# A retention and feed-forward kernel on Trainium2: new orders for its engines, and 13 activation transposes moved from TensorE to DMA

## The chip, the cores and the metric

The kernel runs on one core of a Trainium2 chip. The metric is device time in microseconds (us) of one execution. Before the change the median of three runs is 247.33 us (246.45 to 356.75). The core's engines are TensorE (PE; PEld is its weight load), VectorE (DVE), ScalarE (ACT), GpSimd (POOL) and SyncE (SP); each runs its own instruction list strictly in order. SP issues nearly all DMAs.

## The reference

The first half is retention: attention without softmax, with a decay per head and a causal mask. Its output, laid out as 4608 tokens by 512 features, goes through a feed-forward block with a softmax-weighted activation and a layer norm.

```python
scores = scale * np.matmul(q, k.transpose(0, 1, 3, 2))        # q, k, v: (8, 8, 576, 64) f32
gamma = 1.0 - 2.0 ** (-5.0 - np.arange(H))
ret = scores * np.where(rel >= 0, gamma[:, None, None] ** rel, 0.0)
x = (ret @ v), heads side by side                              # (4608, 512)
h = x @ w_in                                                   # (4608, 1024)
e = np.exp(h - h.max(-1));  solu = h * e / e.sum(-1)
ln = (solu - mean) / np.sqrt(var + 1e-6) * g_ln
out = ln @ w_out                                               # (4608, 512) f32
```

## The kernel before

**Tiles.** The 4608 tokens make 18 windows of 256 tokens. Attention works on 36 half windows `i` (256 tokens, four of the eight heads); the feed-forward block works on 36 tiles `t` of 128 tokens (all features). The kernel's steps have names with the number of the half window or tile behind them:

- SP: `ldq`, `ldk`, `ldv` load f32 inputs (256 KB each) into rings of five buffers; `out` stores a result tile in two or four DMAs.
- POOL: `sq`, `sk` scale q and k by the head's decay (line 308; the first two `sq` are on DVE); `cv` casts v (line 316); `sm` updates the running state `g` (line 441); `sc` casts it to f16 in two halves, `sbd` (line 450); `rs` is the power -0.5 of two tiles' variance (line 530).
- PE: `T` transposes q and k (line 325), `S` makes scores (383), `K` makes the new state term, `I` applies the old state, `V` applies the masked scores (all 348); `M1` is x @ w_in (468), `L` transposes the activation `solu` in eight 128x128 pieces into PSUM (536), `M2` is the product with w_out (560).
- DVE: `mask` (416), `sa` and `sd` (430 to 437, state sums), `em` (479, negated copy of h and its row minimum, the negated maximum), `so` (501, the product of hn and the exponentials, both f32 in SBUF), `x` (519 and 522, the statistics of a window's two tiles at once), `od` (568).
- ACT: `qe`, `xe`, `le` copy the PSUM results of `T`, of `V` and of `L` to SBUF (333, 456, 544); `ex` (491), `va` (510, sum of squares), `oe` (576, scaled result).

**Loops between engines.** The state makes a loop from half window to half window: `K` (PE) to `sa`, `sd` (DVE) to `sm`, `sc` (POOL) to `I` (PE), and the next `K` follows the `V` behind that `I`. A feed-forward tile runs `M1`, `em`, `ex`, `so`, then `L`, `le`, `M2`, `oe`, `out`. Rings limit how far an engine runs ahead: one PSUM buffer each for `xy`, `h_ps`, `o_ps`, `s_ps` and the transposes, three buffers for `solu`, four for `lnT`, three for `o_sb`.

**What sets the order.** `FIRST` holds one list per engine; an engine executes its steps in that order, whatever is ready. `order_ops` merges the five lists by the durations in `DUR` and the rings; this sets the order in which instructions are emitted, and hence which ring buffer each takes. Twelve warm-up products of zeros start PE (line 748); wherever the merge leaves a gap on PE before 31 us and before the first `M2`, further products of zeros are put (`WARM`, line 755).

SP's DMAs use eight semaphores in turn, so that a DMA is issued only once the eighth one before it has landed.

Of the kernel before, what the change touches and what calls it, by code (L numbers as in the profile page):

```python
# [18 lines left out]
    sq=1.03, sk=1.03, st_b=0.4, cast=0.84, rs=0.6, cv=0.61,  # L19
    ld=0.89, ldw=1.34, out=0.72, lm=0.42,  # L20
# [4 lines left out]
WARM = 31.0  # L25
NE = 14
WPOOL = ()

FIRST = dict(
    ACT=(  # L30
        "cv1 cv0 qe0 xe0 qe1 qe2 wi1a wi3a wi2a xe1 wi0a ex0 xe2 qe3 qe4 ex1 le0 xe3 qe5 wg6 va1 "
        "le1 wg2 wg0 wg4 xe4 ex2 nw va0 qe6 xe5 ex3 le2 oe0 va2 ex4 qe7 oe1 va3 qe8 xe6 qe9 xe7 "
        "oe2 le3 va4 ex5 oe3 le4 va5 qe10 xe8 ex6 xe9 le5 oe4 qe12 ex7 ex8 le6 oe5 qe11 xe10 va6 "
        "va7 le7 xe11 ex9 oe6 qe13 va8 va9 oe7 le8 xe12 ex10 qe14 ex11 xe13 le9 va10 oe8 qe15 "
        "ex12 xe14 le10 oe9 va11 qe16 va12 xe15 le11 oe10 ex13 qe17 ex14 qe18 oe11 xe16 va13 le13 "
        "va14 le12 xe17 ex15 qe19 oe13 le14 va15 qe20 ex17 xe18 oe12 qe21 ex16 xe19 oe14 qe22 "
        "va17 le15 va16 ex18 oe15 le16 le17 xe20 oe16 xe21 ex19 va18 qe23 va19 oe17 ex20 le18 "
        "xe22 qe24 ex21 xe23 oe18 le19 va21 le20 va20 oe19 qe25 xe24 ex23 qe26 oe20 xe25 ex22 "
        "le21 va23 qe27 va22 le23 oe21 le22 ex24 qe28 xe26 ex25 xe27 oe22 qe29 va24 va25 ex26 "
        "le24 oe23 qe30 xe28 le25 oe24 qe31 ex27 xe29 oe25 va26 qe32 va27 le26 ex28 le27 xe30 "  # L40
        "ex29 xe31 oe26 qe33 va28 va29 oe27 ex30 le28 ex31 xe32 qe34 xe33 oe28 qe35 va31 le29 "
        "va30 xe34 ex32 le30 xe35 ex33 oe29 va32 va33 ex35 oe30 le31 va35 le32 ex34 oe31 le35 "
        "va34 le34 oe32 oe35 le33 oe34 oe33"
    ),
    DVE=(
        "sq1 sq0 sa0 sd0 mask0 sa1 sd1 mask1 wi1b wi2b sa2 gc sd2 wi3b wi0b mask2 em0 sa3 sd3 so0 "
        "em1 mask3 wg7 so1 sa4 sd4 mask4 em2 wg1 wg5 wg3 mask5 sa5 em3 sd5 so2 x0 wp3 wp0 sa6 od0 "
        "sd6 mask6 em4 so3 od1 em5 sa7 sd7 mask7 so4 x1 od2 sa8 mask8 sd8 em6 od3 so5 sa9 mask9 "
# [12 lines left out]
        "T0 K0 S0 I0 V0 T1 K1 S1 T2 I1 S2 V1 K2 G M1_0 I2 V2 T3 K3 M1_1 T4 S3 L0 I3 V3 S4 K4 T5 "
        "M1_2 L1 I4 V4 K5 S5 M1_3 WM M2_0 T6 I5 V5 K6 S6 L2 M1_4 M2_1 T7 M1_5 I6 T8 V6 K7 S7 M2_2 "
        "T9 I7 V7 S8 K8 L3 M1_6 M2_3 I8 V8 K9 S9 L4 M1_7 T10 M2_4 I9 V9 K10 S10 L5 M1_8 T12 M2_5 "
        "L6 M1_9 T11 I10 V10 K11 S11 M2_6 L7 I11 V11 K12 S12 T13 M1_10 M2_7 I12 L8 V12 S13 K13 "
        "M1_11 T14 M2_8 I13 V13 K14 S14 L9 M1_12 T15 M2_9 L10 I14 V14 S15 K15 M1_13 T16 M2_10 I15 "
        "V15 S16 L11 M1_14 T17 M2_11 T18 I16 S17 V16 M1_15 L13 I17 V17 K18 S18 L12 M2_13 T19 "
        "M1_17 L14 I18 S19 V18 K19 T20 M2_12 M1_16 T21 M2_14 I19 V19 S20 K20 T22 M1_18 L15 I20 "
        "V20 S21 K21 M2_15 L16 M1_19 L17 M2_16 I21 V21 K22 S22 T23 M1_20 M2_17 I22 S23 V22 K23 "
        "L18 M1_21 T24 M2_18 I23 V23 S24 K24 L19 M1_23 L20 M2_19 T25 I24 M1_22 V24 K25 S25 T26 "
        "M2_20 I25 V25 S26 K26 L21 M1_24 T27 M2_21 L23 I26 V26 K27 S27 L22 M1_25 T28 M2_22 I27 "  # L70
        "V27 K28 S28 T29 M1_26 M2_23 L24 M1_27 T30 I28 V28 S29 K29 L25 M2_24 T31 I29 V29 K30 S30 "
        "M2_25 M1_28 T32 I30 V30 S31 K31 L26 M1_29 L27 M2_26 I31 V31 K32 S32 T33 M1_30 M2_27 "
        "M1_31 L28 I32 V32 S33 K33 T34 M2_28 I33 V33 S34 T35 M1_32 L29 I34 S35 V34 L30 M1_33 I35 "
        "V35 M2_29 M1_35 L31 M2_30 M1_34 L32 M2_31 L35 M2_32 L34 M2_35 L33 M2_34 M2_33"
    ),
    POOL=(
        "sk0 sm0 sc0 sk1 sk2 sq2 sm1 sc1 cv2 sm2 sc2 sq3 sk3 cv3 sk4 sq4 sm3 sq5 sc3 cv4 sk5 cv5 "
        "sm4 sc4 sk6 sq6 cv6 sm5 sc5 sk7 sk8 rs0 sq8 sq7 sm6 cv8 sc6 cv7 sq9 sk9 sm7 sc7 cv9 rs1 "
        "cv11 sk10 sm8 sc8 sq12 sq10 cv13 cv10 sm9 sc9 sk12 rs2 sq11 sm10 sc10 sk11 cv12 sq13 "
        "sq16 sk13 sm11 sc11 sq14 sk14 rs3 sm12 sc12 cv14 sm13 sc13 sq15 cv16 sk15 sm14 rs4 cv17 "  # L80
        "sc14 sk16 cv15 cv18 sm15 sc15 sq17 rs5 sk17 sk18 sq18 sq19 sk19 sq21 cv19 rs6 sk21 sk20 "
        "sm18 cv21 sc18 sq20 sq22 sk22 sm19 sc19 cv20 rs7 sm20 sc20 cv22 sk23 rs8 sq23 cv25 sm21 "
        "sk24 sc21 sm22 sq24 cv23 sc22 cv24 sk25 sq25 sm23 rs9 cv26 sc23 sk26 sq26 sm24 sq27 sc24 "
        "rs10 sm25 sc25 sq29 sk27 sm26 cv28 cv29 sc26 cv27 sk28 cv30 sq28 sk29 rs11 sm27 sc27 "
        "sq30 sq31 sk30 sk31 sm28 sc28 rs12 sq32 cv32 sm29 sc29 sq34 sm30 sc30 sk32 cv35 cv31 "
        "sk33 sm31 sq33 sc31 rs13 cv33 sq35 sk34 sm32 sc32 sk35 cv34 sm33 sc33 rs14 rs15 rs16 "
        "rs17"
    ),
    SP=(
        "ldk0 ldq1 ldv1 ldq0 ldv0 ldk1 lm ldv2 ldq2 ldk2 lwi3 lwi1 lwi2 lwi0 ldq3 ldk3 ldv3 ldk4 "  # L90
        "ldq4 ldq5 ldk5 ldv4 lwo6 ldv5 lwo0 lwo2 lwo4 ldk6 ldq6 ldv6 ldk7 ldv7 ldk8 ldq9 ldq8 "
        "ldq7 ldk9 ldv8 ldk10 ldq10 ldv9 out0 ldv11 ldv10 ldk12 ldq12 ldk11 ldv12 out1 ldv16 out2 "
        "ldv13 ldq16 ldq15 ldq13 ldk15 ldk14 out3 ldq11 ldk16 out4 ldk13 ldv17 ldv14 ldq14 ldk17 "
        "out6 ldq17 ldv15 ldq18 out5 ldq22 out7 ldv18 out8 ldk18 ldv21 ldv20 ldq19 ldk21 out9 "
        "ldk19 ldv19 ldk20 ldq21 ldq23 ldv22 ldv23 ldq20 ldk22 out11 out13 out10 ldk25 ldk24 "
        "ldv26 ldv25 ldq26 out12 ldk23 ldk29 ldv24 ldq25 ldv30 ldq24 ldk26 out14 out15 ldq27 "
        "out16 ldq31 ldk28 ldv27 ldv28 ldv29 out17 ldq28 ldv33 out18 ldk27 out19 ldq29 ldk31 "
        "ldq30 ldq32 ldv35 ldv31 ldk30 ldk33 out20 out22 ldq34 ldv32 ldk34 ldk32 out21 ldv34 "
        "ldq35 out23 ldk35 ldq33 out24 out26 out25 out27 out28 out29 out30 out31 out32 out35 "
        "out34 out33"  # L100
# [107 lines left out]
def kernel(  # L208
# [21 lines left out]
               xT=5, h=1, hn=3, e=2, oc=2, solu=3, sq=2, sml=8, lnT=4, o=1, osb=3)  # L230
# [52 lines left out]
    mhalf = small[:, 68:69]  # L283

# [156 lines left out]
    def state_cast(i):  # L443
        w, hf = divmod(i, 2)
        b, wi = wins[w]
        k = n_state[wi]
        n_state[wi] += 1
        s16 = sbd[wi][k % len(sbd[wi])]
        for e in range(2):
            nc.gpsimd.tensor_copy(out=s16[ee[e], :, :, ee[e]], in_=st[i]["g"][ee[e]])  # L450
        cur.setdefault((b, hf), {}).update({"g": st[i]["g"], wi: s16})
# [63 lines left out]
    def stats(w):  # L515
        d = ws[w]
        x = pools["sml"].tile([P, 2], FP, tag="w", name="w")
        d["x2"] = pools["sml"].tile([P, 2], FP, tag="w2", name="w2")
        nc.vector.scalar_tensor_tensor(  # L519
            out=x, in0=d["se"], scalar=1e-6, in1=d["se"], op0=ALU.mult, op1=ALU.mult  # L520
        )
        nc.vector.scalar_tensor_tensor(
            out=d["x2"], in0=d["sv"], scalar=float(DFF) ** -3, in1=x, op0=ALU.mult, op1=ALU.add
        )
# [7 lines left out]
    def ln_tp(t):  # L532
        d = tk[t]
        tp = pools["tp"].tile([P, 8, P], F16, tag="tp", name="tln")
        for c in range(8):
            nc.tensor.transpose(  # L536
                out=tp[:, c], in_=d["solu"][:, c * P : (c + 1) * P], identity=ident
            )
        d["tp"] = tp

    def ln_ev(t):
        d = tk[t]
# [245 lines left out]
```

## Time and profile before

| quantity | value |
|---|---|
| median of three runs | 247.33 us |
| the profiled execution | 246.69 us, span 244.9 us |
| mean granted TensorE clock | 0.992 |
| busy share PE / DVE / ACT / POOL | 88% / 75% / 70% / 71% |
| DMA moved | 42.62 MB, mean 174 GB/s |

The span reaches from the first to the last instruction; 1.8 us of the execution lie around it. The share of busy time is a mean over the whole execution: a fill stage of some 22 us, in which loads and weights arrive, then the stage in which attention and feed-forward steps of different tiles run side by side, then a tail from about 200 us on that is mostly feed-forward work. Matmuls are pipelined: a 128x512 product is recorded with 379 ns, while eight of them in a row take 1.73 us in the chain.

In an answer on one line of code, "x64: 386/398/1453" stands for 64 instructions with their shortest, median and longest time in ns. In the list of waits the three numbers are the total in us, the number of waits and the longest.

### The profile page before, as it was taken

Reading aid. Unit: us, or ns where it says so; the run is one execution under the profiler, and the core shown is the slowest. Engines: PE = TensorE matmul, PEld = TensorE weight load, DVE = VectorE, ACT = ScalarE, POOL = GpSimd, SP = SyncE. Lnnn points to the kernel's source line nnn. Section 1 sums busy time; section 2 is a strip of 40 time slices with the busy share of each in tenths; the row PEclk is TensorE's granted clock in tenths of the full one; section 3 lists DMA queues with packets and bytes.
Section 4 is the critical chain, followed back from the end, with each engine's and each line's share of the span. In section 5 each row is a group of like instructions: output and inputs, shape, how many; then the busy total and the mean of one; then the engine's idle time right before and its main releaser. Section 6 shows DMA issues by size and latency. Waiting matters only on the chain.

```text
span 244.9 us, 7426 instructions
## 1 busy us (share of the span) xinstructions
PE 214.4 (88%) x2998; PEld 124.1 (51%) x2998; DVE 182.9 (75%) x328; ACT 172.2 (70%) x301; POOL 172.7 (71%) x223
## 2 busy tenths in 40 slices
PE   8968887998997788999799889899869999999992
PEld 2435543554554445556456446455445554565550
DVE  7166899887995799989979767849845776897520
ACT  2234786767776597889769685868756687989971
POOL 2097994998959868799968969939995789631020
PEclk9999999999999999999999999999979999999999
DMA  7999999196886065798297865662516550510244
GB/s 188 322 367 300 352 295 269 30 246 170 226 236 185 3 170 175 193 305 237 63 256 196 264 175 136 170 172 82 178 29 188 156 150 4 129 46 23 65 94 120
DMA packets 65633, 42.62 MB, mean 174 GB/s; under 512 B 4024, under 2 KB 59456, under 8 KB 65600
## 3 DMA queue, kind: packets, MB, share of 16 engines
q1 hardware_dynamic: 65200, 41.96, 61.8%
q8 instruction: 23, 0.38, 0.6%
q10 hardware_dynamic: 400, 0.21, 0.4%
q14 instruction: 10, 0.08, 0.1%
HBM read 32.71 MB, written 9.44 MB: 172 GB/s over the span
## 4 chain that ended last, share of the span: by engine, by line
PE 33%; POOL 31%; DVE 13%; DMA 9%; issue 7%; ACT 5%; SPq 1%; POOLq 0%; DVEq 0%; ACTq 0%
POOL sbd L450 9%; PE h_ps L468 8%; POOL k L308 7%; PE o_ps L560 7%; POOL q L308 6%; PE xy L348 6%; POOL g L441 4%; DMA qr<-in_q_dram 4%; POOL v L316 3%; PE tln L536 3%; DVE ret L416 3%; DMA out_dram<-o_sb 2%; PE tqk L325 2%; DVE hn L479 2%; PE wm L755 2%
## 5 line engine op out<-in xcount | busy, mean ns | idle before, releaser
L468 PE MATMUL h_ps<-w_in,xT 128*128 128x512 f16 x288 | 68.8, 382 | 0.9 <-ACT w_in L612 0.9
L501 DVE SCALAR_TENSOR_TENSOR solu<-hn,e_sb 128x1024 f16<-128x1024 f32 x36 | 47.7, 1326 | 5.3 <-ACT e_sb L491 5.3
L479 DVE TENSOR_SCALAR_CACHE_REDUCE hn<-h_ps 128x1024 f32<-128x1024 f32 x36 | 43.8, 1218 | 9.9 <-PE h_ps L468 9.8
L491 ACT ACTIVATE e_sb<-hn,nm 128x1024 f32<-128x1024 f32 x36 | 41.4, 1151 | 8.0 <-DVE hn L479 6.2
L416 DVE TENSOR_TENSOR ret<-s_ps,masks 128x1024 f16<-128x1024 f32 x36 | 43.7, 1215 | 2.5 <-PE s_ps L383 2.5
L308 POOL TENSOR_TENSOR k<-kr,small 128x512 f16<-128x512 f32 x36 | 42.1, 1175 | 4.3 <-DMA kr<-in_k_dram 3.6
L510 ACT ACTIVATE sq<-solu,su 128x1024 f32<-128x1024 f16 x36 | 41.3, 1148 | 1.2 <-DVE solu L501 1.2
L308 POOL TENSOR_TENSOR q<-qr,small 128x512 f16<-128x512 f32 x34 | 39.4, 1165 | 3.7 <-DMA qr<-in_q_dram 3.0
L468 PEld LDWEIGHTS <-xT 128*128 128x128 f16 x288 | 27.0, 99 | 28.7 <-issue 2.0
L560 PEld LDWEIGHTS <-lnT 128*128 128x128 f16 x288 | 26.8, 98 | 28.7 <-issue 0.8
L441 POOL TENSOR_TENSOR g<-tt,small 128x128 f32<-128x128 f32 x32 | 17.1, 534 | 30.7 <-DVE tt L437 30.2
L560 PE MATMUL o_ps<-w2c,lnT 128*128 128x512 f16 x160 | 37.8, 379 | 0.1
L450 POOL CAST sbd<-g 64x256 f16<-64x256 f32 x64 | 34.8, 544 | 3.0
L456 ACT CAST xT<-xy 128x512 f16<-128x512 f32 x36 | 21.0, 584 | 21.3 <-PE xy L348 19.0
L333 ACT COPY qkT<-tqk 128x512 f32<-128x512 f32 x36 | 20.9, 579 | 15.4 <-PE tqk L325 15.3
L530 POOL TENSOR_TENSOR rs<-w,small 128x2 f32<-128x2 f32 x18 | 15.2, 846 | 20.3 <-DVE w L519 12.7
L348 PE MATMUL xy<-qkT,sbd 128*128 128x128 f16 (+1 forms) x128 | 13.5, 214 | 16.4 <-POOL sbd L450 15.8
L316 POOL CAST v<-vr 128x512 f16<-128x512 f32 x34 | 27.1, 801 | 0.8 <-PE xy L348 0.2
L560 PE MATMUL o_ps<-w2g,lnT 128*128 128x512 f16 x112 | 26.5, 379 | 0.6 <-DVE oc L568 0.6
L544 ACT COPY lnT<-tln 128x512 f32<-128x512 f32 x36 | 20.8, 577 | 5.7 <-PE tln L536 5.4
L536 PE MATMUL tln<-ident,solu 128*128 128x128 f16 x288 | 22.1, 220 | 0.5 <-ACT qkT L333 0.4
L536 PEld LDWEIGHTS <-solu 128*128 128x128 f16 x288 | 17.9, 98 | 6.5 <-issue 0.8
(53 smaller groups left out, 260.1 us busy)
## 6 DMA issues: line engine op xcount, KB each, us to landing
kr<-in_k_dram SPq DMA_DIRECT2D x32, 256.0 KB, 5.3
qr<-in_q_dram SPq DMA_DIRECT2D x32, 256.0 KB, 5.1
vr<-in_v_dram SPq DMA_DIRECT2D x32, 256.0 KB, 5.0
out_dram<-o_sb SPq DMA_DIRECT2D x64, 128.0 KB, 2.4
w_in_f<-in_moe_w_in_dram SPq DMA_DIRECT2D x4, 512.0 KB, 6.6
w_f<-in_moe_w_out_dram SPq DMA_DIRECT2D x4, 512.0 KB, 6.6
vr<-in_v_dram SPq DMA_DIRECT2D x16, 64.0 KB, 3.1
qr<-in_q_dram SPq DMA_DIRECT2D x16, 64.0 KB, 2.0
```

The lines of the kernel that those rows point to most:

```text
L308: eng.tensor_tensor(out=t.rearrange("p j h d -> p h j d"), in0=st[i][nm + "r"], in1=g_of(i, base), op=ALU.mult,)
L316: copy(out=t, in_=st[i]["vr"])
L348: nc.tensor.matmul(start=(c, e) not in begun, stop=False, skip_group_check=True, **kw)
L416: nc.vector.tensor_tensor(out=d["ret"].rearrange("p e h j q -> p (e h) (j q)"), in0=d["s"].rearrange("p e h j q -> p (e h) (j q)"), in1=ma ...
L450: nc.gpsimd.tensor_copy(out=s16[ee[e], :, :, ee[e]], in_=st[i]["g"][ee[e]])
L468: nc.tensor.matmul(out=h_ps[:, hh], lhsT=st[2 * w + dc // 2]["xT"][:, c, dc % 2], rhs=w_in16[:, dc, hh], start=(dc == 0), stop=(dc == 3),)
L479: nc.vector.tensor_scalar(out=d["hn"], in0=d["h"], scalar1=-1.0, scalar2=None, op0=ALU.mult, op1=ALU.min, accum_out=d["nm"],)
L491: nc.scalar.activation(out=d["e"], in_=d["hn"], func=ACT.Exp, scale=-1.0, bias=d["nm"], accum_out=ws[w]["se"][:, c : c + 1],)
L501: nc.vector.scalar_tensor_tensor(out=d["solu"], in0=d["hn"], scalar=1.0, in1=d["e"], op0=ALU.mult, op1=ALU.mult, accum_out=ws[w]["su"][:, ...
L510: nc.scalar.activation(out=x, in_=tk[t]["solu"], func=ACT.Square, scale=-float(DFF), bias=ws[w]["su"][:, c : c + 1], accum_out=ws[w]["sv"] ...
L536: nc.tensor.transpose(out=tp[:, c], in_=d["solu"][:, c * P : (c + 1) * P], identity=ident)
L560: nc.tensor.matmul(out=d["o"], lhsT=d["lnT"][:, c], rhs=(w2g16 if t < NE else w2c16)[:, c], start=(c == 0), stop=(c == 7))
```

## The change

It has four parts.

1. All five lists of `FIRST` are new.
2. For tiles 20 to 32 (`XBAR`) step `L` is one DMA with transpose, from `solu` to `lnT`, both in SBUF, issued by SP in the place that `L` has in SP's list. The eight PE transposes and the ACT copy `le` of those 13 tiles go. `M2` of these tiles waits for the DMA, and so does the reuse of the `solu` buffer.
3. `x` is done for each tile by itself with `tensor_scalar`, whose second factor is a column given as a scalar, in place of one `scalar_tensor_tensor` for two tiles with two SBUF tensors; the ring `sml` has 16 buffers in place of 8. `rs` still serves two tiles.
4. The zero products behind the first twelve are 11, at given places (`FILL`), in place of those in the merge's gaps. The table of durations gets two entries (one is for a step that is not used, since `CASTD` is empty).

```diff
-WARM = 31.0
+FILL = dict(T0=2, S0=1, I0=5, T2=1, T3=2)
+XBAR = tuple(range(20,33))
+CASTD = ()
 FIRST = dict(
     PE=(
-        "T0 K0 S0 I0 V0 T1 K1 S1 T2 I1 S2 V1 K2 G M1_0 I2 V2 T3 K3 M1_1 T4 S3 L0 I3 V3 S4 K4 T5 "
...
-        "V35 M2_29 M1_35 L31 M2_30 M1_34 L32 M2_31 L35 M2_32 L34 M2_35 L33 M2_34 M2_33"
+        "G T0 S0 K0 I0 T1 V0 K1 S1 T2 I1 V1 S2 K2 T3 M1_0 I2 V2 K3 S3 M1_1 I3 V3 K4 T4 M1_2 L0 S4 "
...
+        "S34 T35 M1_32 M2_29 I34 S35 V34 M1_33 I35 V35 M2_31 M1_35 L33 M2_30 M1_34 M2_33 L35 "
+        "M2_32 L34 M2_35 M2_34"
     ),
     SP=(
-        "ldk0 ldq1 ldv1 ldq0 ldv0 ldk1 lm ldv2 ldq2 ldk2 lwi3 lwi1 lwi2 lwi0 ldq3 ldk3 ldv3 ldk4 "
...
+        "ldv2 ldk1 ldk0 ldq0 ldk2 ldv0 ldq1 ldv1 lm ldq3 lwi0 ldq2 lwi2 lwi1 ldk3 lwi3 ldv3 ldk4 "
...
+        "out11 ldq27 out13 ldk26 ldv24 ldk24 ldv25 out14 out15 ldq26 out12 ldk27 ldq29 ldv27 "
+        "ldk29 ldk28 ldv26 out16 ldq28 ldq30 ldv28 out17 ldk30 ldq35 L20 ldq31 L21 ldv29 ldq33 "
+        "ldv30 ldv35 ldk31 ldq34 out18 out19 L22 out20 L23 ldk32 out21 ldv31 ldk33 ldk35 L24 L25 "
+        "ldk34 ldq32 out22 ldv33 out24 L26 out23 ldv32 L27 ldv34 L28 L29 out25 out27 out26 L31 "
+        "L30 out29 L32 out28 out30 out31 out33 out32 out35 out34"
     ),
 )
-               xT=5, h=1, hn=3, e=2, oc=2, solu=3, sq=2, sml=8, lnT=4, o=1, osb=3)
+               xT=5, h=1, hn=3, e=2, oc=2, solu=3, sq=2, sml=16, lnT=4, o=1, osb=3)
-    def stats(w):
+    def stats(t):
+        w, c = divmod(t, 2)
         d = ws[w]
-        nc.vector.scalar_tensor_tensor(
-            out=x, in0=d["se"], scalar=1e-6, in1=d["se"], op0=ALU.mult, op1=ALU.mult
-        )
-        nc.vector.scalar_tensor_tensor(
-            out=d["x2"], in0=d["sv"], scalar=float(DFF) ** -3, in1=x, op0=ALU.mult, op1=ALU.add
+        col = slice(c, c + 1)
+        nc.vector.tensor_scalar(
+            out=x, in0=d["se"][:, col], scalar1=d["se"][:, col], scalar2=1e-6,
+            op0=ALU.mult, op1=ALU.mult,
+        )
+        nc.vector.tensor_scalar(
+            out=d["x2"][:, col], in0=d["sv"][:, col], scalar1=float(DFF) ** -3, scalar2=x,
+            op0=ALU.mult, op1=ALU.add,
         )
+    def ln_dma(t):
+        d = tk[t]
+        d["lnT"] = pools["lnT"].tile([P, 8, P], F16, tag="lnT", name="lnT")
+        nc.sync.dma_start(out=d["lnT"], in_=d["solu"], transpose=True)
+        if t in XBAR:
+            op(f"L{t}", "SP", "ldt", [f"so{t}"], (m + 1, 4.9), lambda t=t: ln_dma(t), [("lnT", [f"M2_{t}"])])
+        else:
+            op(f"L{t}", "PE", "L", [f"so{t}"], (m + 1, 4.9), lambda t=t: ln_tp(t), [("tp", [f"le{t}"])])
+            op(f"le{t}", "ACT", "le", [f"L{t}"], (m + 2, 0.97), lambda t=t: ln_ev(t), [("lnT", [f"M2_{t}"])])
```

## The prediction

> **What bounds the kernel now.** I read the page's busy shares first, then the chain that ended last, the groups, the waits, and last the timeline and the windows of two places. No engine is full, and the chain wanders between PE (33%) and POOL (31%):
>
> ```profile
> PE 214.4 (88%) x2998; PEld 124.1 (51%) x2998; DVE 182.9 (75%) x328; ACT 172.2 (70%) x301; POOL 172.7 (71%) x223
> ...
> PE 33%; POOL 31%; DVE 13%; DMA 9%; issue 7%; ACT 5%; SPq 1%; POOLq 0%; DVEq 0%; ACTq 0%
> ...
> L450 POOL CAST sbd<-g 64x256 f16<-64x256 f32 x64 | 34.8, 544 | 3.0
> ...
> L544 ACT COPY lnT<-tln 128x512 f32<-128x512 f32 x36 | 20.8, 577 | 5.7 <-PE tln L536 5.4
> ```
>
> In order of time the chain is POOL and the state loop from 12 us to about 180 us, and almost purely PE from 200 to 240 us. Over 20 to 200 us the windows add up to 158.5 us of PE and 149.5 us of POOL in 180; from 200 to 220 PE has 19.4 of 20. So there are two stages: a loop between engines, then a PE queue.
>
> The answers on single lines show what lengthens the loop:
>
> ```profile
> L450 POOL CAST sbd<-g x64: 386/398/1453, 13.0 to 214.4; 64x256 f16<-64x256 f32 x64
> ...
> L441 POOL TENSOR_TENSOR g<-tt,small x32: 393/399/1379, 12.5 to 213.5; 128x128 f32<-128x128 f32 x32
> ...
> L308 POOL TENSOR_TENSOR k<-kr,small x36: 1036/1042/2108, 4.2 to 210.8; 128x512 f16<-128x512 f32 x36
> ...
> L501 DVE SCALAR_TENSOR_TENSOR solu<-hn,e_sb x36: 1208/1225/2058, 25.9 to 232.5; 128x1024 f16<-128x1024 f32 x36
> ```
>
> Each has a tight median and a longest case about 1 us beyond it; for POOL that is about one `so` of 1.225 us, for `so` about one `sk`. At 204.6 us the timeline has `so` (1.23 us) and `rs` starting together, and `rs` records 1.75 us where its median is 0.689. DVE's product and POOL's work take turns. Count against median over all POOL rows: 175.7 us recorded (42.1 + 39.4 + 27.1 + 17.1 + 34.8 + 15.2) less 144.3 us (36 x 1.042, 34 x 1.042, 34 x 0.609, 32 x 0.399, 64 x 0.398, 18 x 0.689) is 31.4 us of waiting inside POOL instructions. Of it, 13.6 us fall on `sm` and `sc`: (17.1 - 12.8) + (34.8 - 25.5). Those stand in the state loop, and PE pays:
>
> ```profile
> PEld L348 <- POOL sbd L450: 22.0, 20, 3.1
> ...
> PE xy L348 <- POOL sbd L450: 15.8, 17, 2.6
> ```
>
> The exclusive pair itself needs 144.3 + 36 x 1.225 = 188 us between 4 and 236 us, so 44 us of slack are there for a better order; PE is only a little less loaded.
>
> **The parts, against the profiled execution's 246.69 us** (its span is 244.9; 1.8 lie around it; the median shown is 247.33, which is 0.6 above).
>
> *1a. The fill.* T0 starts late only because zero products stand before it:
>
> ```profile
> 7.50 0.69 DVE L308 TENSOR_TENSOR q<-qr,small 128x512 f16<-128x512 f32 x1 [1.63 <-DMA qr<-in_q_dram]
> ...
> 10.92 0.39 PE L325 MATMUL tqk<-ident,q 128*128 128x128 f16 x4
> ```
>
> q0 is fourth in SP's list before and after, and lands at 7.5; `sq0` ends at 8.2, and T0 stood behind 23 zero products until 10.9. k0 goes from first place to third; third place landed at 6.6 (the v cast of 6.58), so `sk0` (1.04 us) ends at 7.6, in time. T0 can start near 8.2. What follows is the first state loop: v0, now sixth, gives `cv0` near 9.8 and K0 with it (11.46 before); `sc0` ends near 12.2 (2.36 us behind K0, as before). POOL then has `sq3`, `cv2`, `sq2` (2.7 us, from loads in places 1, 10 and 12) ahead of `sm1`, `sc1` (1.2 us), which end near 16.6 with q2's landing near 14.3 (18.36 before). xe1 and a weight cast are what M1_0 waits for, as before; it comes at about 19.8 in place of 21.47. **-1.7 us.** Ends: 0 (two more loads are ahead of the weights, at 0.75 us each by the 350 GB/s of that stretch, and `lm`, the masks, moves from seventh to ninth place) and -2.7 (all of T0's gain).
>
> *1b. The clock.* 45 zero products become 23, so PE idles more in the fill. One idle time of that size is in the trace: PE waits 2.58 us until 179.45, and the windows from 180 to 183 show
>
> ```profile
> 181.00:182.00 1.00, 1.00 (x9) 0.86 (x9) 0.99 (x1) 0.80 (x3) 1.00 (x2) 0.50 0.00 0
> ```
>
> half the clock for some 3.9 us; an M1 in it is recorded with 2.59 us in place of 1.89. One such spell costs up to 1.9 us of PE. In the fill PE has little to do, so I take **+1.0**; ends 0 and +3 (T, K, S, I, V of three half windows at half speed, 3 x 1.0 us more). The Trainium skill (TensorE: Matmul & The Clock Gate, Why this matters for your kernels) asks for no idle gaps above about 3 us and speaks of one window of idle; by it the gaps of 1 to 2 us that I expect would cost nothing, while the row says that 2.6 us, after a sparse stretch, were enough.
>
> *1c. The orders in the steady stage.* The trace can't show the new lists' waits. At best no `sm` or `sc` meets a `so`: -13.6 us, all on the loop and near PE's 15.8 us of waiting. At worst the new lists make as many new waits as they remove, and some more: +5 (the longest single waits of PE, POOL on `sd` and DVE are 2.6, 7.2 and 3.6 us; one or two such). POOL and DVE are both over 70% busy, so not every meeting can be avoided; I take half, **-6.8**.
>
> *2. L by DMA.* Removed: 13 x 8 transposes, 0.45 us per tile in the chain, and 13 `le` at 0.577 us (7.5 us of ACT). PE is the queue from 199.5 us on; the last ten L stand there, in the old list those of tiles 26 to 35 (the order at its end is L31, L32, L35, L34, L33), so seven of the thirteen are on the path: **-3.2**. The other six (2.7 us) lie where PE has idle time; I count none, and -5.9 is the end. Behind the last M1 the old list keeps PE 5 x 1.73 + 4 x 0.45 = 10.45 us, the new one 4 x 1.73 + 2 x 0.45 = 7.8: these are part of the same 3.2, with one M2 moved ahead. Late next is then em, ex, so, L, le, M2 of tile 34 (5.9 us from M1's end to M2_34 by the old timeline), against 6.1 us of PE work before it: balanced.
>
> Added: 13 DMAs on SP, each a hop of its own between `so` and M2. Nothing like them is in the trace. Nearest rows, 256 KB each as here:
>
> ```profile
> kr<-in_k_dram SPq DMA_DIRECT2D x32, 256.0 KB, 5.3
> ...
> qr<-in_q_dram SPq DMA_DIRECT2D x16, 64.0 KB, 2.0
> ```
>
> Cheap end 2.0 us to landing (the smallest row), dear end 19 us: the queue's 65200 packets took 61.8% of 16 x 244.9 us, 37 ns each, and in 32-byte pieces there would be 8192, over 16 engines. I take 5.3. M2 can stand it: between so20 and M2_20 the PE list holds some 14 us of work. Tighter is the `solu` ring of three: so25 needs tile 23's buffer. L23 stands behind out20 on SP, and so it is issued about 3.6 us after M2_20's end (the `oe` 0.7, a transpose, two stores 1.1), while so25 is ready some 7.5 us after it (T28, four attention steps, M2_21 and M1_25 are 4.8, em25 1.3, ex25 1.35). 5.3 us are too long by 1.4 there, with DVE 25% idle to take it up: **+0.5** for all such places; ends 0 and, at 19 us, +24 by the second rival's price. What is queued behind an L that waits: on SP the loads and stores (L29 ahead of out25, L31 ahead of L30 and out29). Loads are far ahead (after the fill POOL hardly waits for one), and no store there is needed within its L's wait.
>
> The Trainium skill (VectorE: DVE Perf Modes, The three transpose paths) speaks against this edit: 390 ns on TensorE against 1309 ns by DMA for one 128x128. Eight in series would be an estimated 10.5 us; no row shows it. With it, L23 would be late by 6.6 us in place of 1.4; with the 0.5 grown in proportion, to 2.4, the sum would be 238.4.
>
> *3. x by tile.* 36 old instructions recorded 12.5 us, 5.2 at their shortest of 0.144. Now 72; the nearest row, the `tensor_scalar` of `gln`, took 0.157: 11.3 us if nothing blocks them, 25 us at the old 0.35. That is -1 to +12 us of DVE, not on the path but near 200 us; **0**.
>
> Sum: 246.7 - 1.7 + 1.0 - 6.8 - 3.2 + 0.5 = **236.5 us**.
>
> **Rivals.**
>
> *The orders bring nothing* (the change doesn't do what it says). For it: nothing holds an engine back when the other runs; the lists only fix a sequence, and each of POOL's six rows can meet `so` at another place. Then 236.5 + 6.8 + 1.0 (part of 1a lost in the same waits) = 244.3, within 2%.
>
> *The transposes are slow*; the slower side. Place: `so(t+3)`, through the ring of three. Three tiles last 3 x 5.9 = 17.7 us (M1 from 21.5 to 229.3 over 35 tiles); `so` takes 1.3 and SP's queue some 3 (four 32-partition loads took 2.03), so it decides from 13.4 us to landing on. Price: 13/3 x (landing - 13.4); at 18 us +20, or 256. For it: the dear end, and that they share a queue with 40 MB of loads. Against: 256 KB usually land in 5.3 us. The 2% line is crossed at 17 us.
>
> *A dearer loop*: the worst end of 1c, 236.5 + 11.8 = 248.3, and 250.3 with 1b at its end.
>
> **How the numbers follow.** Forecast 0.57 (own range 229 to 242), orders bring nothing 0.22 (244), slow transposes 0.15 (256), dearer loop 0.06 (250). Low end of the range: 1a and 2 at their best with 11 of 1c's 13.6 give 246.7 - 2.7 - 5.9 - 11 + 0.5 = 228; all at its best at once is left out, some 0.05. High end: 254 takes in the dearer loop and leaves out the upper two thirds of the slow transposes, 0.1. 2%, about what a measurement of this kernel can tell from no change, is 242.4 to 252.3 around the median. Faster is the forecast's 0.57; within 2% are 0.22 and a third of the dearer loop, 0.24; slower are 0.15 and the rest of it, 0.19.
>
> **What would show it.** Right: T0 near 8.2 and M1_0 near 20 us; the means of `sbd` and `g` near 0.45 us (0.54 now); PE's waits for `sbd` halved; the DMA issues' row for `lnT` at 4 to 7 us; no wait of DVE's `so` on a landing above 2 us; PE's last product 2.5 us closer to the last M1. Wrong: `sbd`'s mean unchanged; `lnT` landing above 13 us with `so` or M2 waiting for it; clock 0.5 in the slices behind 8 us, with M1_0 no earlier than before; SP late with stores so that `oe` waits for its buffers.

## The result, and the profile after

The changed kernel takes **229.74 us** (median; fastest 227.68), the kernel before 247.82 us beside it: ratio **0.9255 [0.918, 0.9331]**. In a second set of runs the pair gave 230.75 against 247.15 us, ratio 0.932 [0.9249, 0.939]. The forecast was 236.5 us, so the time lies in its range, but the gain is 16 to 18 us where 10 to 11 were expected. The profiled execution takes 227.68 us (span 225.9, granted clock 1.0); it is the shortest of them. The medians given as measured take in every execution; the ratios, the table of experiments 3 and 4 and the differences of experiments 6 and 8 leave out those over 1.5% longer than the kernel's fastest.

The page of the changed kernel, the same rows as shown of before (line numbers have moved: `sbd` 450 to 451, `g` 441 to 442, `so` 501 to 504, the state products 348 to 349):

```profile
PE 200.7 (89%) x2872; PEld 115.4 (51%) x2872; DVE 182.9 (81%) x364; ACT 165.7 (73%) x288; POOL 167.5 (74%) x223
...
PE 38%; POOL 22%; DMA 14%; SPq 10%; ACT 5%; DVE 4%; issue 4%; ACTq 0%; POOLq 0%; DVEq 0%
...
L451 POOL CAST sbd<-g 64x256 f16<-64x256 f32 x64 | 31.4, 490 | 2.8
...
L442 POOL TENSOR_TENSOR g<-tt,small 128x128 f32<-128x128 f32 x32 | 17.2, 536 | 6.8 <-DVE tt L438 5.2
```

and the row of the new DMAs in the list of DMA issues, which ends with the median us from issue to landing:

```profile
lnT<-solu SPq DMA_TRANSPOSE x13, 3.3
```

POOL's share of the chain falls from 31% to 22%; DMA and SP's queue grow in it from 9% and 1% to 14% and 10%. The means of `sbd` and `g`, which the prediction wanted at 0.45 us, hardly move: 0.544 to 0.490 and 0.534 to 0.536. The answers on single lines:

```profile
L451 POOL CAST sbd<-g x64: 387/401/1387, 12.0 to 195.5; 64x256 f16<-64x256 f32 x64
...
L442 POOL TENSOR_TENSOR g<-tt,small x32: 393/400/1380, 11.6 to 194.6; 128x128 f32<-128x128 f32 x32
...
L504 DVE SCALAR_TENSOR_TENSOR solu<-hn,e_sb x36: 1209/1292/1986, 27.2 to 214.0; 128x1024 f16<-128x1024 f32 x36
```

DVE's product and POOL's pieces still meet. Count against median over `sm` and `sc` is (17.2 - 32 x 0.400) + (31.4 - 64 x 0.401) = 10.1 us, 13.6 before. But the waits say that fewer of these meetings reach PE:

```profile
PEld L349 <- POOL sbd L451: 11.6, 13, 2.1
PE xy L349 <- POOL sbd L451: 8.4, 12, 1.6
```

15.8 us of PE's waiting for `sbd` have become 8.4. POOL's own wait for DVE's `tt` fell from 30.2 to 5.2 us, and DVE's for PE's `h_ps` from 9.8 to 1.9.

**Where the 19.0 us between the two profiled executions lie.** The row of M1 gives its first and last start, here before the change and then after it:

```profile
L468 PE MATMUL h_ps<-w_in,xT x288: 376/379/634, 21.5 to 229.3; 128*128 128x512 f16 x144
```

```profile
L471 PE MATMUL h_ps<-w_in,xT x288: 376/379/390, 19.3 to 211.1; 128*128 128x512 f16 x144
```

The start is 2.2 us shorter, the stretch from the first M1 to the last 16.0 us (207.8 to 191.8), and what follows it, up to the end of the span, 0.8 us (15.6 to 14.8). So nearly all of it comes out of the middle. There the windows from 20 to 200 us, before and then after (PE's busy time first), show the same PE doing 10 us more work in 180:

```profile
20.00:200.00 180.00, 158.50 (x2367) 93.93 (x2366) 147.04 (x251) 130.78 (x228) 149.45 (x187) 0.99 0.67 187
```

```profile
20.00:200.00 180.00, 168.47 (x2520) 98.92 (x2519) 160.32 (x307) 141.17 (x247) 153.53 (x201) 1.00 0.79 207
```

### The profile page after: what moved, and what is told of

Its sections match the earlier page's. It is cut to its first block, busy times and chain, and to the rows that moved or that the text cites. A ratio compares the mean times of both kernels' runs of the same rounds, so it can differ in the third digit from the quotient of the medians.

```text
span 225.9 us, 7231 instructions
## 1 busy us (share of the span) xinstructions
PE 200.7 (89%) x2872; PEld 115.4 (51%) x2872; DVE 182.9 (81%) x364; ACT 165.7 (73%) x288; POOL 167.5 (74%) x223
## 4 chain that ended last, share of the span: by engine, by line
PE 38%; POOL 22%; DMA 14%; SPq 10%; ACT 5%; DVE 4%; issue 4%; ACTq 0%; POOLq 0%; DVEq 0%
PE o_ps L574 14%; PE h_ps L471 12%; POOL sbd L451 6%; PE xy L349 6%; DMA vr<-in_v_dram 6%; SPq L294 4%; DMA w_f<-in_moe_w_out_dram 4%; POOL k L309 4%; POOL v L317 4%; DMA w_in_f<-in_moe_w_in_dram 3%; POOL q L309 3%; POOL g L442 3%; PE tqk L326 3%; POOL rs L539 3%; ACT xT L459 2%
## 5 line engine op out<-in xcount | busy, mean ns | idle before, releaser
L309 POOL TENSOR_TENSOR k<-kr,small 128x512 f16<-128x512 f32 x36 | 45.0, 1257 | 13.0 <-DMA kr<-in_k_dram 11.2
L504 DVE SCALAR_TENSOR_TENSOR solu<-hn,e_sb 128x1024 f16<-128x1024 f32 x36 | 49.5, 1379 | 2.6 <-ACT e_sb L494 2.4
L309 POOL TENSOR_TENSOR q<-qr,small 128x512 f16<-128x512 f32 x34 | 36.9, 1090 | 0.9 <-DMA qr<-in_q_dram 0.3
L451 POOL CAST sbd<-g 64x256 f16<-64x256 f32 x64 | 31.4, 490 | 2.8
L539 POOL TENSOR_TENSOR rs<-w,small 128x2 f32<-128x2 f32 x18 | 16.3, 904 | 20.5 <-DVE w L530 10.2
L334 ACT COPY qkT<-tqk 128x512 f32<-128x512 f32 x36 | 20.8, 579 | 13.7 <-PE tqk L326 13.6
L317 POOL CAST v<-vr 128x512 f16<-128x512 f32 x34 | 24.6, 725 | 7.2 <-DMA vr<-in_v_dram 6.8
L442 POOL TENSOR_TENSOR g<-tt,small 128x128 f32<-128x128 f32 x32 | 17.2, 536 | 6.8 <-DVE tt L438 5.2
L590 ACT ACTIVATE o_sb<-o_ps,rs 128x512 f32<-128x512 f32 x20 | 13.7, 687 | 8.7 <-POOL rs L539 3.6
L326 PE MATMUL tqk<-ident,q 128*128 128x128 f16 x144 | 14.0, 220 | 3.1 <-DVE q L309 2.2
L349 PEld LDWEIGHTS <-sbd 128*128 128x128 f16 x128 | 8.3, 98 | 15.4 <-POOL sbd L451 11.6
```

The lines of the kernel that those rows point to most:

```text
L309: eng.tensor_tensor(out=t.rearrange("p j h d -> p h j d"), in0=st[i][nm + "r"], in1=g_of(i, base), op=ALU.mult,)
L317: copy(out=t, in_=st[i]["vr"])
L349: nc.tensor.matmul(start=(c, e) not in begun, stop=False, skip_group_check=True, **kw)
L451: (nc.vector if i in CASTD else nc.gpsimd).tensor_copy(out=s16[ee[e], :, :, ee[e]], in_=st[i]["g"][ee[e]])
L504: nc.vector.scalar_tensor_tensor(out=d["solu"], in0=d["hn"], scalar=1.0, in1=d["e"], op0=ALU.mult, op1=ALU.mult, accum_out=ws[w]["su"][:, ...
```

## The experiments

Line numbers below are each kernel's own. Ratios are against the kernel before on the same chip. Experiments 1 to 4 ran on one chip (before: 246.47 us), 5 to 8 on another (247.17), 9 and 10 with the changed kernel again on a third (247.15), 11 on a fourth (247.36).

**1. All of the change but the DMA transposes.**

```diff
-XBAR = tuple(range(20,33))
+XBAR = ()
-        "ldk29 ldk28 ldv26 out16 ldq28 ldq30 ldv28 out17 ldk30 ldq35 L20 ldq31 L21 ldv29 ldq33 "
+        "V23 S24 K24 L19 M1_23 T25 M2_18 T26 I24 S25 V24 K25 L20 M1_22 L21 M2_19 I25 V25 K26 S26 "
+        "le19 va19 qe25 va21 qe26 ex23 oe18 le20 xe24 va20 le21 oe19 xe25 va23 ex22 qe27 oe20 ex24 "
```

The lines are one each of SP's, PE's and ACT's lists; the other tiles go the same way.

> The new orders with all 36 L on TensorE again: the 13 transposes by DMA are undone, and the 13 L and le are put back into the lists of PE and ACT where they fit best. Theory A (the prediction's: seven of thirteen L on the path): 229.7 + 3.2 = 233 us. Rival B (with the new lists PE has hardly a gap anywhere, so each L counts): 13 x 0.45 = 5.9 us and more, 235.6 to 237 us. Rival C (the DMA transposes are most of the whole gain): 240 us or more.

Measured: 229.65 us, 0.9339 [0.9282, 0.9395], below all three expectations. By medians the DMA transposes are worth nothing (229.65 us without them, 229.74 and 230.75 with them), by ratios 0.2% (against the second pair above) to 0.8%. The orders, with the fill and x, give nearly everything.

PE is busy 206.9 us here and 200.7 in the changed kernel, but its idle time is 20.9 us here (of a span of 227.8) and 25.2 there. POOL's waits for loads, which bear on part 2, are here

```profile
POOL k L308 <- DMA kr<-in_k_dram: 7.5, 4, 5.0
...
POOL v L316 <- DMA vr<-in_v_dram: 6.1, 4, 3.4
```

and in the changed kernel

```profile
POOL k L309 <- DMA kr<-in_k_dram: 11.2, 4, 5.3
...
POOL v L317 <- DMA vr<-in_v_dram: 6.8, 4, 3.3
```

**2. The DMA transposes alone.** `L20` to `L32` are put into the old SP list where their `so` is ready; all else as before.

```diff
+XBAR = tuple(range(20, 33))
+        if t in XBAR:
+            op(f"L{t}", "SP", "ldt", [f"so{t}"], (m + 1, 4.9), lambda t=t: ln_dma(t), [("lnT", [f"M2_{t}"])])
...
-        "out16 ldq31 ldk28 ldv27 ldv28 ldv29 out17 ldq28 ldv33 out18 ldk27 out19 ldq29 ldk31 "
+        "ldv27 ldv28 ldv29 out17 L20 ldq28 L21 ldv33 out18 ldk27 out19 ldq29 ldk31 ldq30 ldq32 L23 "
```

> The old orders, with only the 13 L moved to DMA (the thirteen L and le leave the lists of PE and ACT, the DMAs go into SP's list where so is ready). Theory A: seven L leave the PE queue of the tail, 247.8 - 3.2 = 244.6 us; the orders are the larger part of the gain. Rival C: 240 us or less, the orders bring little. If the transposes hold up SP's loads and stores: 247 us or more.

Measured: 249.7 us, 1.0059 [1.0014, 1.0105], a small loss. The profiled execution is a long one (250.34 us, the ten lie between 245.8 and 251.78), with 13.7 us at half clock where the kernel before had 3.4. PE's 13 x 8 transposes are gone, but its busy time is no less (214.7 us, 214.4 before) and its idle time is more (33.8, 30.5 before). The timeline of PE near 204 us:

```profile
207.73 0.29 PE L346 MATMUL xy<-qkT,sbd 128*128 128x128 f16 x2 [3.89 <-POOL sbd L448]
```

and the chain of that time:

```profile
201.77 3.59 DMA qr<-in_q_dram
205.35 0.07 issue
205.42 1.46 POOL q L306
206.88 0.35 POOL sbd L448
```

A load of q, issued at 201.77 behind loads, stores and transposes on SP, holds `sq`, `sc` and with them PE for 3.89 us. That the 0.6% is lost in this place in the other executions is not shown.

**3 and 4. The exclusion taken away, before and after.** The product of two SBUF tensors becomes one that reads a single tensor.

```diff
-        nc.vector.scalar_tensor_tensor(
-            out=d["solu"], in0=d["hn"], scalar=1.0, in1=d["e"], op0=ALU.mult, op1=ALU.mult,
+        nc.vector.tensor_scalar(
+            out=d["solu"], in0=d["e"], scalar1=1.0, scalar2=None, op0=ALU.mult, op1=ALU.add,
```

> The kernel before with the product's operands changed: so reads only the exponentials (tensor_scalar times 1.0 with the sum), not hn; the output is another one, the instruction has the same size. With one SBUF input it should not exclude GpSimd, and every POOL row's mean falls to its median (0.40 for sbd and g, 1.04 for k). Theory A (the waits of sm and sc behind so are 13.6 us of the loop, and the new orders took half of it away): about 236 us, and the same step in the changed kernel brings half as much. Rival B (the orders' gain has little to do with the exclusion): the same step brings about as much in the changed kernel as here.

> The changed kernel with the same product of one SBUF input (another output, the same size). Theory A: the new orders have already put the products beside harmless POOL work, so at most -3 us, about 227 us. Rival B: the exclusion costs as much as in the kernel before, -6 us or more, 224 us or less.

Measured: in the kernel before 234.12 us, 0.9431 [0.9356, 0.9506]; in the changed kernel 226.0 us, 0.9154 [0.9085, 0.9222]. The answers on the two lines in the kernel before with one tensor read:

```profile
L501 DVE TENSOR_SCALAR_CACHE_REDUCE solu<-e_sb x36: 1203/1210/1221, 26.5 to 220.6; 128x1024 f16<-128x1024 f32 x36
...
L450 POOL CAST sbd<-g x64: 388/398/861, 13.6 to 202.5; 64x256 f16<-64x256 f32 x64
```

The product lasts as long as at its shortest before, but its longest case, 2.06 us, is gone, and POOL's six rows add up to 146.3 us in place of 175.7: the prediction counted 144.3 from medians. So it is this product's second operand from SBUF that shuts POOL out. `mask`, which also multiplies two tensors, but has one of them in PSUM, is never lengthened in the kernel before:

```profile
L416 DVE TENSOR_TENSOR ret<-s_ps,masks x36: 1209/1214/1225, 12.7 to 219.2; 128x1024 f16<-128x1024 f32 x36
```

Medians on that chip, with the new orders taken from experiment 1:

| | two tensors read | one tensor read | price of the exclusion |
|---|---|---|---|
| old orders | 246.43 | 233.47 | 12.96 |
| new orders | 229.65 | 224.71 | 4.94 |
| gained by the new kernel | 16.78 | 8.76 | 8.02 |

(The last cell of the new orders also has the DMA transposes, which moved nothing in experiment 1. By the intervals of the ratios each difference is sure to some 2 us. The product that leaves out `hn` may also free `hn`'s buffers sooner, which no run here separates.) One tensor read brings 13.0 us in the old orders and 4.9 in the new, nearer to theory A (half as much) than to B (as much). About half of the gain, 8 us, is there only while this product's exclusion is. The other half does without it: with one tensor read the old lists are still 8.8 us slower, and POOL waits even longer for DVE's `tt` there (37.3 us, 30.2 before). Which of the old lists' waits make up that half, no run here separates.

**5. The fill of before in the changed kernel.**

```diff
-FILL = dict(T0=2, S0=1, I0=5, T2=1, T3=2)
+FILL = dict(T0=14, S0=1, I0=5, T2=1, T3=2)
```

> The changed kernel with 14 zero products ahead of T0 instead of 2, as many as before the change; all else as changed. The changed kernel stands at 229.74 us (ratio 0.9255). Step 1a of the prediction (the fill is on the path at the start): T0 starts about 2.7 us later, at 10.9 us instead of 8.2, M1_0 near 21.5 instead of 19.3, and the whole takes 1.7 to 2.2 us longer, 231.4 to 232. Rival (the start is set by the loading of the weights and by GpSimd's first pieces, and the fill only stands beside them): M1_0 moves by less than 0.5 us and the time stays within 0.5 us, 229.3 to 230.2. Step 1b (the clock): the granted clock is 1.0 from the start in both, and so no part of a difference is the clock's.

Measured: 231.64 us, 0.9288 [0.9137, 0.944]; too wide to tell. T0 starts at 9.15 us, not at 10.9 as expected. M1 starts at 21.47 us, as it did before, but the profile (of an execution of 235.27 us) has 6.8 us of half clock from 15.7 us on, so the shift isn't the fill's alone. Experiment 10 does it the other way round.

**6. x once for a window.**

```diff
-    def stats(t):
+    def stats(w):
...
-        nc.vector.tensor_scalar(
-            out=x, in0=d["se"][:, col], scalar1=d["se"][:, col], scalar2=1e-6,
-            op0=ALU.mult, op1=ALU.mult,
+        nc.vector.scalar_tensor_tensor(
+            out=x, in0=d["se"], scalar=1e-6, in1=d["se"], op0=ALU.mult, op1=ALU.mult
```

> The changed kernel with x computed once for a window of two tiles, as before the change, at the place where the second tile's x stood; all else as changed. Step 3 of the prediction (x by tile costs VectorE alone, off the path, and its one-input form shuts nobody out): VectorE is busy some 3 us less, and the time stays within 1 us of 229.7. Rival 1 (the two-input form meets GpSimd's pieces at 18 more places): the means of GpSimd's groups g and sbd rise from 0.536 and 0.490 us and the time rises by 1 to 3 us. Rival 2 (the first tile of a window now gets its x later, and M2 waits for the second): PE waits at M2 and the time rises by 2 us or more.

Measured: 233.65 us, 0.9445 [0.9323, 0.9566]; by ratios 1.3% and 1.9% slower than the changed kernel's two, with intervals that overlap, so likely slower and not shown. First x in this kernel, then in the changed one:

```profile
L520 DVE SCALAR_TENSOR_TENSOR w<-se x18: 149/315/1016, 41.1 to 224.0; 128x2 f32<-128x2 f32 x18
```

```profile
L526 DVE TENSOR_SCALAR w<-se x36: 197/205/210, 41.8 to 215.2; 128x1 f32<-128x1 f32 x36
```

With two tensors read, x itself has to wait for POOL, up to 0.87 us; as `tensor_scalar` it never does. `g` rises to a mean of 0.597 us, as the first rival said. The largest loss is one place, in POOL's timeline (v waits for its load, and then v and `g` both meet a `so`):

```profile
188.76 1.46 POOL L315 CAST v<-vr 128x512 f16<-128x512 f32 x1 [2.75 <-DMA vr<-in_v_dram]
190.18 1.37 POOL L440 TENSOR_TENSOR g<-tt,small 128x128 f32<-128x128 f32 x1
```

PE stands still 3.47 us for it, and from 0.7 us behind that, 3.41 us run at half clock. Whether this loss belongs to x, or to lists that were drawn up with the other x, this run can't tell.

**7. SP's list in the order in which its steps become ready.**

```diff
-        "ldq13 ldv8 ldv9 ldv7 ldk9 ldk12 ldq11 ldv13 ldk10 ldq12 ldq10 ldk11 out0 ldv11 ldk15 "
-        "out1 ldq14 ldv10 ldk13 ldk16 out3 out4 ldk14 ldv12 out5 ldq15 ldk17 out2 ldq18 ldq20 "
+        "ldv8 ldv9 ldv7 ldk9 ldk12 ldq11 ldv13 ldk10 ldq12 ldq10 ldk11 ldv11 ldk13 ldv10 out0 ldv12 "
```

> The changed kernel with SyncE's list, from the first store on, put in the order in which its steps became ready in the changed kernel's trace, so that loads no longer stand behind stores whose data come later; all else as changed. GpSimd waits there 11.2 us for loads of k and 6.8 us for loads of v. Theory D (these waits are on the path now, and are what the new orders left): both fall below 3 us, and the time falls by 3 to 6 us, to 224 to 227. Theory E (GpSimd has this much slack, since its own idle time is only moved): the waits fall but the time stays within 1 us, 228.7 to 230.7, and GpSimd waits for scalar pieces or buffers instead.

Measured: 229.07 us, 0.9286 [0.9213, 0.9359]. GpSimd's wait for v falls from 6.8 to 0.6 us, and that for k to 7.6, of which 4.9 are the first load; the time does not fall. By its number this is theory E. But the timeline of PE shows a place where time was given back:

```profile
163.92 3.21 PE L573 MATMUL o_ps<-w2c,lnT 128*128 128x512 f16 x8 [3.45 <-DMA lnT<-solu]
```

This is `M2_22`. PE was ready for it at 160.47 us, 1.5 us earlier than in the changed kernel, which starts it at 161.99, and then waited for its transposed tile, issued at 159.0 and landed 4.9 us later; the M2 itself ran mostly at half clock, 3.21 us in place of 1.89.

**8. Twelve more tiles by DMA**, with the list of experiment 7.

```diff
-XBAR = tuple(range(20,33))
+XBAR = tuple(range(8,33))
```

> The kernel with SyncE's list by readiness, and the transposes of the activation by DMA for tiles 8 to 32 instead of 20 to 32 (twelve more). Step 2 of the prediction (each transpose that TensorE gives up saves up to 0.45 us on its path): TensorE's busy time falls by a further 5 us, and the time by up to 5 us against the same kernel without the twelve, so 219 to 226. Rival (the products are paced by GpSimd's and VectorE's pieces, as moving the thirteen by itself showed, and TensorE only idles more): the time is within 1 us of the kernel without the twelve, and PE's idle time grows by what its busy time loses. Second rival (the transposing DMAs crowd SyncE's queue in the middle, where loads are due): GpSimd's waits for k, q and v rise above 10 us, and the time rises by 2 us or more.

Measured: 237.29 us, 0.9431 [0.9277, 0.9586]: by ratio 1.5% slower than without the twelve, or 3.7 us of median, which rests on two executions here (231.43 and 234.04 us); the intervals overlap, so that it is slower is likely and not shown. The profile is of an execution of 240.53 us. In it landings take 4.0 us (median) and up to 6.0. PE is busy no less than in experiment 7 (205.3 us, 203.7 there), with 23.9 us at half clock, and waits for the landings:

```profile
PE o_ps L572 <- DMA lnT<-solu: 7.9, 2, 4.1
```

The gain of up to 5 us did not come, and neither rival holds as written: GpSimd's waits for loads did not rise; in the profiled execution the transposes hold PE itself.

**9. SP's list sorted, transposes on TensorE.** SP's list sorted as in experiment 7, but from experiment 1's trace, in the kernel of experiment 1; beside it the changed kernel again.

```diff
-XBAR = tuple(range(20,33))
+XBAR = ()
...
-        "out1 ldq14 ldv10 ldk13 ldk16 out3 out4 ldk14 ldv12 out5 ldq15 ldk17 out2 ldq18 ldq20 "
+        "ldv8 ldv9 ldv7 ldk9 ldk12 ldq11 ldv13 ldk10 ldq12 ldq10 ldk11 ldv11 ldk13 ldv10 out0 ldv12 "
```

> The changed kernel itself, beside the two others of this call on one chip. It had 229.74 us, ratio 0.9255 [0.918, 0.9331]; the same is expected, 0.922 to 0.933. For the clock: in the ten traces so far the granted clock of TensorE changes only on a grid of 3.413 us, whose place differs from one execution to the next; in no trace did a cell of that grid with over 2.05 us of busy TensorE go before a cell at half clock, and nearly every cell with under 1.45 us did. The wait of 2.21 us before T0 lay across two cells there (2.01 and 2.05 us busy) and cost nothing. Theory F (it is the place of the grid that decides): in this execution the same wait, if it falls into one cell, is followed by a cell at half clock, and the time is some 1.5 to 2 us longer; if it lies across two again, the clock stays 1.0. Rival (the length of the wait decides): the clock stays 1.0 wherever the grid lies.

> The changed kernel with the transposes of the thirteen tiles back on TensorE and ScalarE (as in the run with the transposes on TensorE, 229.65 us, ratio 0.9339), and SyncE's list sorted by the times at which its steps became ready there. With the sorted list and the transposes by DMA, TensorE reached the middle earlier, and then waited 3.44 us for one transposed tile at 160.5 us, followed by 3.41 us at half clock. Theory G (that transpose gave back what the earlier loads had won): without it the time falls to 224 to 227 us, ratio 0.905 to 0.918. Rival (the loads are not what is late; GpSimd's and VectorE's pieces pace the middle): the time stays at 229 to 231.

Measured: the changed kernel 230.75 us, 0.932 [0.9249, 0.939]; this one 228.58 us, 0.9266 [0.9213, 0.9318]. Theory G expected 224 to 227, its rival 229 to 231; it lies between. By ratio it is 0.5% below the changed kernel and 0.7% below experiment 1, less than the intervals can tell apart, so SP's waits cost little here. The windows of this kernel name the next bound; below them the same window of experiment 1:

```profile
140.00:200.00 60.00, 59.44 (x874) 35.64 (x864) 49.65 (x100) 50.81 (x92) 46.09 (x66) 1.00 0.46 119
```

```profile
140.00:200.00 60.00, 59.43 (x906) 36.20 (x905) 49.63 (x100) 50.90 (x91) 47.69 (x66) 1.00 0.50 134
```

PE is busy 59.4 of 60 us in both (57.2 in the changed kernel): with the transposes on it PE is full there, whichever list SP has, and a better list of loads can win nothing in that stretch.

**10. The new fill alone**, in the kernel before.

```diff
-                if fill and 6.0 < start[o.name] < WARM:
-                    for _ in range(int((start[o.name] - end_pe - 0.3) / 0.36)):
+                for _ in range(FILL.get(o.name, 0)):
```

> The kernel before with the zero products of the changed kernel alone (11 behind the first twelve, at given places, instead of 33 in the gaps of the merge); orders, transposes and x as before. Step 1a of the prediction (T0 stands behind zero products, and the start is on the path): T0 starts near 8.2 us instead of 10.9, the first M1 1 to 2 us earlier than 21.47, and the whole is 1.5 to 2 us shorter, ratio 0.992 to 0.994. Step 1b (fewer zero products cost clock): cells at half clock in the first 40 us, and the whole is 0 to 2 us longer. Rival (the first loads and GpSimd's pieces set the first M1, and what is won at the start is waited off behind it): ratio 0.998 to 1.002.

Measured: 246.13 us, 0.9963 [0.9923, 1.0003]. T0 starts at 8.20 us, M1 at 18.99 in place of 21.47; the whole gains about 1 us. Windows of this kernel:

```profile
16.84:20.25 3.41, 1.57 (x27) 0.86 (x15) 2.69 (x7) 1.66 (x4) 2.24 (x4) 1.00 1.16 290
20.25:23.66 3.41, 3.41 (x31) 1.88 (x30) 1.23 (x2) 1.00 (x1) 3.41 (x5) 0.50 0.96 267
```

3.41 us at half clock follow a spell in which PE was busy 1.57 us of 3.41.

**11. More zero products in the fill**, in the kernel of experiment 9.

```diff
-FILL = dict(T0=2, S0=1, I0=5, T2=1, T3=2)
+FILL = dict(T0=4, S0=1, I0=9, T2=3, I1=2, T3=2)
```

> The kernel of the run with SyncE's list sorted and the transposes on TensorE (228.58 us, ratio 0.9266 [0.9213, 0.9318]), with eleven more zero products in TensorE's idle times before the first M1: 4 instead of 2 ahead of T0, 9 instead of 5 ahead of I0, 3 instead of 1 ahead of T2, 2 ahead of I1. A zero product takes about 0.25 us there, and the idle times at these places were 0.63, 1.39, 0.56 and 0.64 us, so no step is meant to start later. Theory F (a cell of the 3.413 us grid with little busy TensorE makes the next one run at half clock): no cell before the first M1 has under 2.1 us of busy TensorE, so none of the first 25 us is at half clock, wherever the grid lies; there the run without them had one cell at half clock from 16.5 us. The time falls by 0 to 1.5 us, to 227 to 228.6, and differs less from run to run. Rival (half clock at the start comes of something else): a cell at half clock in the first 25 us again, and the same time, 228.2 to 230.7.

Measured: 228.16 us (five of six runs within 227.62 to 228.43), 0.9225 [0.9181, 0.9268]. The start had no half clock, although one cell held only 1.89 us of PE work, less than was meant. It is the fastest kernel here that computes the same output. Its median is 1.6 and 2.6 us below the changed kernel's two, but the intervals overlap, so that it beats the changed kernel is likely and not shown.

## Why the prediction was right in direction and too small

*1a and 1b, fill and clock* (-1.7 and +1.0, together -0.7). Right: experiment 10 measured the two together at -1.0 by medians, with the end of the interval at no change. T0 came at 8.22 us (8.2 forecast), M1 at 19.3 (19.8). The clock's share differs between executions (last section): the profiled one after lost none, its repetition ran 3.4 us at half speed. The spell that the step read from the trace of before as some 3.9 us lasts 3.41 us, from 179.70 to 183.11.

*1c, the orders* (-6.8, with 0 to -13.6 and +5 as ends). This is the term that failed, in size and in reason. The step read the lengthening inside `sm` and `sc` as the most that the orders could give, and took half because "not every meeting can be avoided". Only a quarter was (13.6 to 10.1 us), yet the middle became 16 us shorter; by experiments 1 and 10 the orders, with the new x, are worth about 16 us (16.8 less some 1 for the fill), more than the best end. Two things were missing. The lengthening does not price a meeting: over all POOL rows before it was 31.4 us and cost 13.0 in time (experiment 3); in the changed kernel the rows hold 26.7 us more than their medians (171.4 recorded, 144.7 from medians), and the new orders pay 4.9 (experiments 1 and 4). And the lists differ in more than their meetings: 8.8 us come without this product's exclusion, and what they come from stays open.

*2, L by DMA* (-3.2 + 0.5). Too much. 6.2 us of PE's work do go (206.9 to 200.7 us busy between experiment 1 and the changed kernel), but the time gains 0 to 0.8%, and with the old orders loses 0.6%. The count of seven on the path was made on the old list; with the new ones and the transposes on it, PE is busy 59.43 of the 60 us from 140 to 200 (experiment 9), so it isn't for want of a full PE that the saving failed. The tail did not pay either. PE's last product was to end 2.5 us closer to the last M1; it ended 0.7 us closer (10.4 us from end to end, then 9.7), since PE waits there for an ACT copy that stands behind a wait for `rs`:

```profile
217.05 0.61 PE L545 MATMUL tln<-ident,solu 128*128 128x128 f16 x8 [1.70 <-ACT lnT L558]
```

With all transposes on PE, in experiment 1, it is 8.6 us. The failed sentence is the one on SP, "Loads are far ahead (after the fill POOL hardly waits for one), and no store there is needed within its L's wait." In the changed kernel POOL waits for late loads, on the chain at 178 to 183 us:

```profile
178.43 0.16 SPq L553
178.59 0.04 issue
178.63 0.59 SPq L602
179.22 0.04 issue
179.26 0.59 SPq L602
179.85 0.04 issue
179.90 3.37 DMA vr<-in_v_dram
183.27 0.06 issue
183.32 0.61 POOL v L317
```

A load of v stands behind a transpose and two stores. SP is held about 1.27 us by each transpose, a cost that the sum did not have. But the transposes are only part of it: POOL waits 18.0 us for loads of k and v in the changed kernel, 13.6 in experiment 1, which has the new lists without the transposes, and 3.6 in the kernel before. So most of the late loads come with SP's new list, and 4.4 us with the transposes; PE's waits for `sbd` are 8.4 and 6.7 us. Whether that is all that ate the saving is not shown. The landing, 5.3 us by the nearest row, was 3.3; the place that was to cost 0.5, `so25` behind L23, did not show as a wait.

*3, x by tile* (0). 15.1 us for 72 instructions, 0.21 us each where 0.157 was assumed; on DVE's account as forecast (12.5 before). That the form also spares POOL and itself the exclusion was not counted; undoing it cost 2 to 3 us of median in experiment 6, with the reserve made there.

*The rivals.* "The orders bring nothing" falls with experiment 1. "The transposes are slow" falls in the changed kernel (3.0 to 5.0 us to landing, against 13.4 from which it was to decide), though its mechanism, a transposed tile that comes late, is what PE waits for in the profiles of experiments 7 and 8, through M2 and not through `so`. "A dearer loop" falls with the windows.

## What to carry to other kernels

Where two engines shut each other out, price it with a run that takes away the shared resource, not by the time recorded inside their instructions: 31 us of lengthening cost 13 here, and 27 us under other orders 5. Moving work from a full engine to a DMA need not pay: 6.2 us of PE's work went and at most 0.8% of the time with it; look first at the loads and stores behind it in the queue, and at who waits for the transfer itself. And a wait of TensorE can cost more than its length when half clock follows it.

## What the runs showed of the hardware

**The clock moves on a grid.** In all 14 traces the granted TensorE clock changes only at steps of 3.413 us, and the place of that grid differs between executions; a cell is one such step. Two executions of the changed kernel, cut at their own grid; first the one of 227.68 us, then that of 230.06 us:

```profile
4.00:7.41 3.41, 2.01 (x9) 0.64 (x7) 0.59 (x4) 0.00 (x0) 0.84 (x1) 1.00 1.09 293
7.41:10.82 3.41, 2.04 (x44) 1.31 (x45) 1.17 (x3) 1.10 (x2) 2.65 (x3) 1.00 1.19 305
```

```profile
6.44:9.86 3.42, 1.64 (x17) 0.79 (x20) 0.93 (x1) 0.70 (x2) 2.50 (x3) 1.00 1.18 299
9.86:13.27 3.41, 3.13 (x37) 1.29 (x37) 2.30 (x5) 1.02 (x2) 1.19 (x3) 0.50 1.09 346
```

In the first an idle spell of 2.21 us lies across two cells (2.01 and 2.04 us busy) and costs nothing. In the second the longest spell there is only 1.32 us, but it and smaller ones fall into one cell (1.64 us busy), and the next cell runs at half clock. Over all cells of the 14 traces: with under 1.45 us of busy PE 26 of 26 were followed by half clock (14 of them are the ends of the traces, where PE's work is over), from 1.45 to 2.05 us 9 of 39, above that 3 of 877, and those three were themselves at half clock. So the 2.58 us by which the prediction judged such a spell was no threshold. The busy share of a cell tells more than the length of a spell, though between 1.45 and 2.05 us it doesn't decide; and so two executions of one kernel can differ by where the grid lies.

**Which instructions of DVE and POOL take turns.** `scalar_tensor_tensor` on two SBUF tensors met POOL even at 128x2; the `tensor_scalar` of experiment 3, at 128x1024, and that of x, at 128x1, were never lengthened (1203 to 1221 ns, 197 to 210 ns), nor was `mask`. But one tensor from SBUF does not always go free. The scaling of w_out, a `tensor_scalar` of 128x512 from f32 to f16, before the change:

```profile
L616 DVE TENSOR_SCALAR w2g<-w_f,gln x4: 593/811/1258, 29.8 to 37.0; 128x512 f16<-128x512 f32 x4
```

In experiment 3 nine POOL instructions still last over 0.1 us longer than their median, and each overlaps this one, the cast of w_in (also 128x512 from f32 to f16) or `w2c`, a product of two SBUF tensors. What sets these one-tensor forms apart from the others, no run here separates.

**A transposing DMA** of 128x1024 f16 from SBUF to SBUF holds SP for 1.27 us (median; 0.54 to 0.58 us for the DMA of a 256 KB load) and lands after 3.0/3.3/5.0 us with 13 of them, 3.0/4.0/6.0 with 25.
